# Moving the output stores of seven batches from SyncE's queue to GpSimd's, in a one-core attention and expert kernel

## The chip, the core and the metric

The kernel runs on one core of a Trainium2 chip. The metric is device time in microseconds (us) of one launch, the median of several executions. Engines are named PE (TensorE), DVE (VectorE), ACT (ScalarE), POOL (GpSimd) and SP (SyncE). A DMA is issued from one engine's queue, and a queue takes its instructions in order: an instruction that waits holds back everything behind it on that engine.

## What is computed

There are 8 batches of 576 tokens. Attention (8 heads of 64) first lets 32 learned packs per head attend to the keys and values, and then lets the queries attend to the packed values. The 512 columns that come out per token go to one of 8 experts (two layers, 512 to 1024 to 512), picked per token by a gate, with the previous token's expert kept where a local gate says so:

```python
p_packed = sm_attn(p, k, v)
out = sm_attn(q, p_packed, p_packed)
...
e = fresh_e if s == 0 or local_gate[b, s] < 0.5 else prev_e
h = np.maximum(x[b, s] @ w1[e], 0.0)
out[b, s] = p[e] * (h @ w2[e])
```

## The kernel before

The kernel computes a whole batch with the expert of its first token, and ends with a branch for batches in which some token needs another expert; in the profiled execution the branch isn't taken.

For each batch the second attention's output stays in its factors: weights `a2t` (packs by tokens) and the packed values, which are multiplied into w1 by `pack_weights` (L976), so that layer 1 (L1019) multiplies the attention weights with packed expert weights. Products are made of high and low float32r parts: `a2h` and `a2l` of the attention weights (L688 on ACT, L691 on POOL), `wph` and `wpl` of w1, two halves of `w2s` for w2 (L1005 on ACT, L1007 on DVE, in batch 1 and most of batch 0 on POOL), and two halves of `h` (L1030 on ACT, L1034 on DVE).

Layer 1 and layer 2 run in two halves of the tokens (320 and 256), each over 8 chunks of 128 of the 1024 hidden columns. Layer 2 of a chunk (L1052, L1057, L1061) comes one chunk after its layer 1, and sums in PSUM banks over the 8 chunks. After the last chunk each output block is scaled into a tile `o` and stored (`store`, L1066 to L1101): blocks 0, 1 and 4 at the end of the first half, blocks 2 and 3 at the end of the second. Blocks 0 to 3 are 128 rows of 512 float32 (256 KB), block 4 is 64 rows (128 KB). `o` has 5 buffers. The last batch has other blocks (`LAST_BLOCKS`), cut into smaller stores.

Beside these two layers, PE works ahead on the next batches: scores against the keys (L509), packed values (L573), scores of the queries (L624), the gate (L803, L811), and `pack_weights`. The expert of a batch is found early, in `first_choice` and `first_code` (L755 to L760): DVE writes its number to `e0`, SP reads that into a register (L760, a TENSOR_LOAD) and then issues the expert's w1 in two loads of 1 MB (L926) and w2 in eight of 256 KB (L897). POOL reads the same number (L835), and copies the expert's code to `v0` (L836), which DVE needs for `sel` (L846) in `gates`.

All loads and, before the change, all stores but one of the last batch are issued by SP. Nothing is scheduled on the chip: the order of each engine's instructions is made while the program is built. Generators (`loads`, `weights`, `store`, `gates` and so on) yield the tiles and slots that they need, `weave` steps the one that is due, and a class `Clock` keeps the time at which each engine and each tile would be ready. `Clock.note` books every instruction: a DMA from SP on a resource "DMA" with a rate, a DMA from ACT on a second resource "DMA2" that SP's loads don't share.

Of the kernel before, what the change touches and what calls it, by code (L numbers as in the profile page):

```python
# [19 lines left out]
B, H, S, D = 8, 8, 576, 64  # L20
# [40 lines left out]
class Clock:  # L61
# [71 lines left out]
    def note(self, inst):  # L133
        outs = [x.bass_ap for x in inst.outs if hasattr(x, "bass_ap")]
        ins = [x.bass_ap for x in inst.ins if hasattr(x, "bass_ap")]
        if inst.opcode == "TensorLoad":

            if "SP" in str(inst.engine):
                self.until["SP"] = self.ready([x for x in ins]) + 1000.0
        if not outs:  # L140
            return
        dma = inst.opcode == "DMACopy"
        if dma:
            aside = "Activation" in str(inst.engine)
            kind, took = "DMA2" if aside else "DMA", min(x.free_size() * x.partition_size() for x in outs + ins if x.space != DRAM) * 4 / self.rate
        else:
            kind, took = self.price(inst, outs, ins)
        start = max(self.engine(kind), self.engine("Activation" if aside else "SP") if dma else 0.0)
        for x in ins + ([] if dma else [y for y in outs if y.tensor.name not in self.apart]):
            at, by = self.written.get(self.key(x), (0.0, kind))  # L150
            start = max(start, at + (LAT if by != kind else 0.0 if kind == "PE" else SAME))
        for x in outs:
            t = x.tensor.name
            start = max(start, 0.0 if dma or t in self.apart else self.used.get(self.key(x), 0.0))
            if t in self.before:
                start = max(start, self.used.get(self.before.pop(t), 0.0) + LAT)
        if kind == "Pool" or kind == "DVE" and inst.opcode in ("TensorTensor", "TensorScalar", "TensorScalarPtr") and not any(x.space == PSUM for x in ins + outs):
            for a, z in self.port["DVE" if kind == "Pool" else "Pool"][-8:]:
                if a <= start < z:
                    start = z  # L160
            self.port[kind].append((start, start + took))
        end = start + took
        self.until[kind] = end
        if dma:
            end += 2000.0 if start < 25000.0 else 2500.0
        for x in outs:
            if x.tensor.name in self.apart:
                end = max(end, self.written.get(self.key(x), (0.0, kind))[0])
        for x in outs:
            self.written[self.key(x)] = (end, kind)  # L170
        for x in ins + outs:
            for t in {x.tensor.name, self.key(x)}:
                self.used[t] = max(end, self.used.get(t, 0.0))
# [3 lines left out]
def packed_attn_moe_kernel(  # L177
# [12 lines left out]
    nc = tc.nc  # L190
# [7 lines left out]
    def tile_(shape, dtype, name, tag=None):  # L198
        bufs = BUFS.get(tag or name, 2)
        x = sb.tile(shape, dtype, name=name, tag=tag or name, bufs=bufs)  # L200
        clock.follow(x.tensor.name, tag or name, bufs)
        return x
# [68 lines left out]
    def at(src, b):  # L271

        return src[b] if isinstance(b, int) else src[bass.ds(b, 1)].squeeze(0)
# [8 lines left out]
    def give(*tiles):  # L282
        clock.done.update(x.tensor.name for x in tiles)

    def need(*tiles, slot=(), banks=0, when=None, by=("Activation", "DVE"), first=False, tiled=False):
        slots = [(x, 1) if isinstance(x, str) else x for x in ((slot,) if isinstance(slot, str) else slot)]

        def ready():

            if (when is not None and not when()) or not all(clock.free_slot(*x) for x in slots):  # L290
                return None
            free = free_banks()
            if len(free) < banks + (hold[0] if banks and not first else 0):
                return None
            return max(clock.ready(tiles), free[banks - 1][0] if banks else 0.0, *(clock.slot(*x) for x in slots))
        ready.banks, ready.by, ready.tiled = banks, by, tiled
        return ready
# [742 lines left out]
    def columns(st, i):  # L1040

        return slice(0, DM) if 5 not in st["blocks"][1] or i not in (3, 5) else slice(0, 256) if i == 3 else slice(256, DM)
# [23 lines left out]
    def store(b, st, i, mask=None):  # L1066

        acc, pe = st["acc", i], st["pe"]
        yield need(acc)
        o = tile_([128, DM], F32, "o")  # L1070
        cols, n = columns(st, i), min(i, 3) if i != 4 else 4
        row, rows = ROWS[n]
        if i == 4:

            o2 = tile_([TAIL, DM], F32, "o2", "o")
            nc.scalar.activation(out=o2, in_=acc[TAIL:128], func=AF.Copy, scale=pe[TAIL:128, i:i + 1])
            yield need(o2)
            nc.vector.scalar_tensor_tensor(
                out=o[:TAIL], in0=acc[0:TAIL], scalar=pe[0:TAIL, i:i + 1], in1=o2, op0=ALU.mult, op1=ALU.add,
            )  # L1080
        elif i == 0:

            nc.scalar.activation(out=o[:, 0:256], in_=acc[:, 0:256], func=AF.Copy, scale=pe[:, i:i + 1])
            nc.vector.tensor_scalar(out=o[:, 256:DM], in0=acc[:, 256:DM], scalar1=pe[:, i:i + 1], scalar2=None, op0=ALU.mult)
        elif n == 3:
            nc.scalar.activation(out=o[:, cols], in_=acc[:, cols], func=AF.Copy, scale=pe[:, 3:4])
        else:
            nc.vector.tensor_scalar(out=o, in0=acc, scalar1=pe[:, i:i + 1], scalar2=None, op0=ALU.mult)
        give(acc)
        dst = at(out, b)[row:row + rows]  # L1090
        if mask is not None:
            new, o = o, tile_([128, DM], F32, "o")
            nc.sync.dma_start(out=o[:rows], in_=dst)
            nc.vector.copy_predicated(
                out=o[:rows], mask=mask[:rows, i:i + 1].broadcast_to([rows, DM]), data=new[:rows],
            )
        queue = nc.scalar if i == 5 else nc.sync
        clock.rate = 300.0
        step = rows // 2 if st["blocks"] is LAST_BLOCKS and i in (0, 1, 2, 4) else rows
        for z in range(0, rows, step):  # L1100
            queue.dma_start(out=dst[z:z + step, cols], in_=o[z:z + step, cols])  # L1101
# [173 lines left out]
    with tc.If(stray_reg > 0, label="none_stray"):  # L1275
# [42 lines left out]
        with tc.For_i(0, B) as bi:  # L1318
            with tc.For_i(0, E) as ei:
                go = nc.values_load(todo[0:1, bass.ds(bi, 1), bass.ds(ei, 1)].rearrange("a b e -> a (b e)"), min_val=0, max_val=1)  # L1320
                with tc.If(go > 0):
                    st = {}
# [44 lines left out]
```

## Time and profile before

| | us |
|---|---|
| runs shown, median of 3 | 416.08 |
| runs shown, each | 416.15, 416.08, 412.57 |
| the profiled execution, its own time | 413.3 |
| its span, first to last instruction | 411.5 |
| PE busy / DVE / ACT / POOL | 403.7 / 298.4 / 180.3 / 45.6 |
| mean granted TensorE clock | 1.000 (2.4 GHz) |

The span is what the trace covers; 1.8 us of the profiled execution's time lie outside it. The batches repeat with a period near 47.5 us from 171 us on. Times below are counted from the start of the span. "Idle before" is the time in which an engine waited for the instruction shown, with what released it. Instructions that issue DMAs appear on a queue (SPq), with the time that the issue took.

### The profile page before, as it was taken

Reading aid. Unit: us, or ns where it says so; the run is one execution under the profiler, and the core shown is the slowest. Engines: PE = TensorE matmul, PEld = TensorE weight load, DVE = VectorE, ACT = ScalarE, POOL = GpSimd, SP = SyncE. Lnnn points to the kernel's source line nnn. Section 1 sums busy time; section 2 is a strip of 40 time slices with the busy share of each in tenths; the row PEclk is TensorE's granted clock in tenths of the full one; section 3 lists DMA queues with packets and bytes.
Section 4 is the critical chain, followed back from the end, with each engine's and each line's share of the span. In section 5 each row is a group of like instructions: output and inputs, shape, how many; then the busy total and the mean of one; then the engine's idle time right before and its main releaser. Section 6 shows DMA issues by size and latency. Waiting matters only on the chain.

```text
span 411.5 us, 10035 instructions
## 1 busy us (share of the span) xinstructions
PE 403.7 (98%) x3811; PEld 319.3 (78%) x3817; DVE 298.4 (73%) x905; ACT 180.3 (44%) x440; POOL 45.6 (11%) x67
## 2 busy tenths in 40 slices
PE   7999999999999999999999999999999999999996
PEld 4657777778878788778887788787786788878895
DVE  4497679994969939698687868787695886867231
ACT  3555533643435425455244534364254453454221
POOL 2004400722030000300011000300003000200000
PEclk9999999999999999999999999999999999999999
DMA  7979999999994995859984899829998400744022
GB/s 205 273 266 294 150 168 293 171 280 135 145 364 145 180 168 99 302 153 198 132 256 157 264 132 159 322 87 224 137 139 301 154 2 2 256 141 130 0 65 57
DMA packets 169325, 73.08 MB, mean 178 GB/s; under 512 B 135088, under 2 KB 149424, under 8 KB 169272
## 3 DMA queue, kind: packets, MB, share of 16 engines
q1 hardware_dynamic: 168660, 72.11, 79.1%
q8 instruction: 31, 0.51, 0.6%
q10 hardware_dynamic: 612, 0.28, 0.3%
q14 instruction: 22, 0.18, 0.2%
HBM read 62.94 MB, written 9.44 MB: 176 GB/s over the span
## 4 chain that ended last, share of the span: by engine, by line
PE 84%; DMA 6%; DVE 4%; SPq 3%; issue 1%; ACT 1%; ACTq 0%; DVEq 0%
PE bank L1052 39%; PE bank L1019 22%; PE bank L1057 4%; DMA w1t<-in_moe_w_dram 4%; PE bank L1061 3%; PE bank L976 3%; PE bank L573 2%; PE bank L509 2%; PE bank L624 2%; PE bank L547 2%; DMA p_in<-in_p_dram 1%; PE bank L803 1%; SPq L352 1%; DMA qt<-in_k_dram 1%; SPq L350 1%
## 5 line engine op out<-in xcount | busy, mean ns | idle before, releaser
L1052 PE MATMUL bank<-w2s,h 128*128 128x512 f32 (+1 forms) x792 | 204.3, 392 | 0.5 <-DVE h L1034 0.5
L1052 PEld LDWEIGHTS bank<-w2s,h 128*128 128x128 f32 x792 | 137.3, 188 | 24.4 <-issue 1.7
L1034 DVE SCALAR_TENSOR_TENSOR h<-bank,h 128x256 fp32r<-128x256 f32 x192 | 61.1, 346 | 51.8 <-ACT h L1030 50.7
L1030 ACT ACTIVATE h<-bank 128x256 fp32r<-128x256 f32 (+1 forms) x128 | 52.6, 411 | 104.2 <-PE bank L1019 102.4
L1019 PEld LDWEIGHTS bank<-a2h,wph 128*128 128x128 f32 x256 | 46.6, 188 | 15.4 <-issue 1.8
L1019 PE MATMUL bank<-a2h,wph 128*128 128x320 f32 (+1 forms) x256 | 55.8, 299 | 0.1
L691 POOL TENSOR_TENSOR a2l<-a2t,a2h 128x576 fp32r<-128x576 f32 (+2 forms) x17 | 22.4, 1321 | 297.7 <-ACT a2h L688 297.4
L1019 PE MATMUL bank<-a2h,wpl 128*128 128x320 f32 (+1 forms) x256 | 54.3, 293 | 0.0
L1019 PE MATMUL bank<-a2l,wph 128*128 128x320 f32 (+1 forms) x256 | 54.3, 293 | 0.0
L1019 PEld LDWEIGHTS bank<-a2h,wpl 128*128 128x128 f32 x256 | 40.8, 188 | 0.0
L1019 PEld LDWEIGHTS bank<-a2l,wph 128*128 128x128 f32 x256 | 40.8, 188 | 0.0
L1005 ACT CAST w2s<-w2raw 128x512 fp32r<-128x512 f32 x64 | 37.3, 618 | 1.9 <-DMA w2raw<-in_moe_w_dram 1.7
L1007 DVE TENSOR_TENSOR w2s<-w2raw,w2s 128x512 fp32r<-128x512 f32 x50 | 32.2, 683 | 0.3 <-ACT w2s L1005 0.2
L1057 PE MATMUL bank<-w2s,h 128*128 128x512 f32 x64 | 27.1, 424 | 0.0
L1061 PE MATMUL bank<-w2s,h 128*64 128x512 f32 x64 | 25.3, 395 | 0.0
L644 DVE STREAM_TRANSPOSE sT<-bank 128x288 f32<-128x288 f32 (+2 forms) x36 | 13.1, 418 | 10.2 <-ACT gate L642 9.5
L608 DVE STREAM_TRANSPOSE qn<-qn 128x1152 f32<-128x1152 f32 x14 | 19.2, 1370 | 1.1 <-DMA qn<-in_q_dram 1.0
L1007 POOL TENSOR_TENSOR w2s<-w2raw,w2s 128x512 fp32r<-128x512 f32 x14 | 17.8, 1292 | 15.9 <-ACT w2s L1005 13.0
L989 ACT CAST wph<-bank 128x512 fp32r<-128x512 f32 x28 | 14.7, 598 | 11.0 <-PE bank L976 11.0
L517 DVE TENSOR_SCALAR_CACHE_REDUCE a<-bank 128x288 f32<-128x288 f32 x32 | 13.3, 452 | 5.8 <-PE bank L509 5.8
L992 DVE TENSOR_TENSOR wpl<-bank,wph 128x512 fp32r<-128x512 f32 x28 | 17.3, 669 | 0.0
L476 DVE STREAM_TRANSPOSE qn<-qn 128x1152 f32<-128x1152 f32 x12 | 16.4, 1368 | 0.0
(158 smaller groups left out, 452.2 us busy)
## 6 DMA issues: line engine op xcount, KB each, us to landing
w2raw<-in_moe_w_dram SPq DMA_DIRECT2D x64, 256.0 KB, 6.9
w1t<-in_moe_w_dram SPq DMA_DIRECT2D x14, 1024.0 KB, 7.1
kv<-in_v_dram SPq DMA_DIRECT2D x16, 512.0 KB, 6.1
qn<-in_q_dram SPq DMA_DIRECT2D x28, 288.0 KB, 7.3
out_dram<-o SPq DMA_DIRECT2D x28, 256.0 KB, 3.6
qn<-in_k_dram SPq DMA_DIRECT2D x24, 288.0 KB, 6.0
w1t<-in_moe_w_dram SPq DMA_DIRECT2D x4, 512.0 KB, 3.5
out_dram<-o SPq DMA_DIRECT2D x14, 128.0 KB, 2.4
```

The source lines that it names most:

```text
L476: nc.vector.transpose(out=kT, in_=kT)
L608: nc.vector.transpose(out=qT, in_=qT)
L691: eng.tensor_tensor(out=a2l, in0=a2t, in1=a2h.bitcast(F32), op=ALU.subtract)
L992: nc.vector.tensor_tensor(out=lo[fh][:, Q], in0=ts[fh, Q], in1=hi[fh][:, Q].bitcast(F32), op=ALU.subtract)
L1005: nc.scalar.copy(out=w[:, 0], in_=raw)
L1007: (nc.gpsimd if st["pick"] and not st["early"] or st["early"] and c > 1 else nc.vector).tensor_tensor(out=w[:, 1], in0=raw, in1=w[:, 0].bi ...
L1019: nc.tensor.matmul(out=t[:, :GROUP * (m1 - m0)], lhsT=st["wp"][c // 4][wi][:, Q, fs], rhs=a2[ai][Q][:, GROUP * m0:GROUP * m1], start=(n == ...
L1030: nc.scalar.activation(out=h[:, :w], in_=t[:, :w], func=AF.Relu)
L1034: nc.vector.scalar_tensor_tensor(out=h[:, dst:dst + z - a], in0=t[:, a:z], scalar=0.0, in1=h[:, a:z].bitcast(F32), op0=ALU.max, op1=ALU.su ...
L1052: nc.tensor.matmul(out=acc[:, cols], lhsT=hs[hi], rhs=w[:, wi, cols], start=(c == 0 and n == 0), stop=(c == NC - 1 and n == 2),)
L1057: nc.tensor.matmul(out=acc, lhsT=h[:, 256:WIDE + TAIL], rhs=w[:, 0], start=(c == 0), stop=False, skip_group_check=True,)
L1061: nc.tensor.matmul(out=acc[0:TAIL], lhsT=h[:, 256:WIDE], rhs=w[:, 1], start=False, stop=(c == NC - 1), skip_group_check=True,)
```

## The change

Stores of batches 0 to 6 are issued from POOL's queue; those of the last batch and of the branch stay where they were. These are 35 stores, 28 of 256 KB and 7 of 128 KB. The second edit books them in the planner on "DMA2" and after POOL's own time, where they were on "DMA" after SP's.

```diff
         if dma:
-            aside = "Activation" in str(inst.engine)
+            aside = next((x for x in ("Activation", "Pool") if x in str(inst.engine)), None)
...
-        start = max(self.engine(kind), self.engine("Activation" if aside else "SP") if dma else 0.0)
+        start = max(self.engine(kind), self.engine(aside or "SP") if dma else 0.0)
...
-        queue = nc.scalar if i == 5 else nc.sync
+        queue = nc.scalar if i == 5 else nc.gpsimd if 0 <= st["at"] < B - 1 else nc.sync
```

On SP the three stores of batch 5's first half stood between the load of a later batch's queries (L368) and the register load of batch 6's expert (L760). SP's rows there before:

```order
L368 DMA qn_4155<-in_k_dram 32x72x32 x4
L368 DMA qn_4198<-in_q_dram 32x72x32 x4
L1101 DMA out_0_dram<-o_4493 128x512
L1101 DMA out_0_dram<-o_4499 128x512
L1101 DMA out_0_dram<-o_4513 64x512
L760 TENSOR_LOAD e0_4518
L760 ISA x2
L926 ISA
L926 DMA w1t_4551<-in_moe_w1_dram 128x4x512
```

SP's rows at the same place now:

```order
L368 DMA qn_4164<-in_k_dram 32x72x32 x4
L368 DMA qn_4202<-in_q_dram 32x72x32 x4
L760 TENSOR_LOAD e0_4518
L760 ISA x2
L926 ISA
L926 DMA w1t_4551<-in_moe_w1_dram 128x4x512
```

The register load and the w1 loads now follow directly on the query loads; otherwise SP's loads keep their order, in this place and in the others.

POOL's rows around the gate of batch 2 before (`a2l` are the low parts of batch 2's attention weights, `e0_1800` its expert's number, `v0_2016` the code that DVE's `sel` of batch 2 reads):

```order
L691 TENSOR_TENSOR a2l_1377<-a2t_1373,a2h_1375 128x576
L691 TENSOR_TENSOR a2l_1378<-a2t_1374,a2h_1376 128x576
L835 TENSOR_LOAD e0_1800
L835 ISA x2
L836 ISA
L836 COPY v0_2016<-code_82 128x1
L837 COPY v0_all_114<-v0_2016 128x1
```

POOL's rows there now (`o_1834`, `o_1843` and `o_1854` are blocks 0, 1 and 4 of batch 1, `o_2098` and `o_2109` its blocks 2 and 3):

```order
L1101 DMA out_0_dram<-o_1834 128x512
L1101 DMA out_0_dram<-o_1843 128x512
L1101 DMA out_0_dram<-o_1854 64x512
L691 TENSOR_TENSOR a2l_1377<-a2t_1373,a2h_1375 128x576
L691 TENSOR_TENSOR a2l_1378<-a2t_1374,a2h_1376 128x576
L1101 DMA out_0_dram<-o_2098 128x512
L1101 DMA out_0_dram<-o_2109 128x512
L835 TENSOR_LOAD e0_1800
L835 ISA x2
L836 ISA
L836 COPY v0_2016<-code_82 128x1
```

The copy of `v0` now stands behind two stores, each of which waits for its `o`; from batch 2 on every batch has this order. On DVE the three rows `o_2098` (L1088), `ex` (L844) and `sel` (L846) follow on one another in both kernels. From batch 3 on, the planner also places `pack_weights` and its neighbours on PE one half-step of layer 2 earlier; PE's instructions are the same in number.

## Rows read from the trace of the kernel before

**Rows 1.** The page's first part: busy time and share of each engine, instructions.

```profile
PE 403.7 (98%) x3811; PEld 319.3 (78%) x3817; DVE 298.4 (73%) x905; ACT 180.3 (44%) x440; POOL 45.6 (11%) x67
```

**Rows 2.** Stretches: length, busy us of PE, PEld, DVE, ACT, POOL, PEclk, DMA share, GB/s.

```profile
75.00:125.00 50.00, 49.51 (x486) 39.68 (x486) 39.61 (x108) 22.71 (x56) 15.71 (x16) 1.00 1.14 210
125.00:173.00 48.00, 48.00 (x430) 38.80 (x432) 36.85 (x110) 20.57 (x51) 3.18 (x4) 1.00 0.84 190
...
268.00:318.00 50.00, 49.40 (x487) 39.71 (x480) 38.63 (x114) 22.67 (x55) 3.19 (x4) 1.00 0.88 182
...
365.00:411.50 46.50, 42.55 (x253) 37.42 (x251) 20.46 (x63) 14.09 (x32) 0.00 (x0) 1.00 0.22 61
```

**Rows 3.** Who PE's matmuls waited for: us in total, times, longest.

```profile
PE bank L976 <- DMA w1t<-in_moe_w_dram: 0.6, 1, 0.6
PE bank L1052 <- DVE h L1034: 0.5, 1, 0.5
```

**Rows 4.** Timeline of SP's queue before batch 6's w1: start, us, engine, line, operation.

```profile
301.41 4.21 SPq L1101 DMA_DIRECT2D out_dram<-o  x3
306.69 1.02 SPq L926 DMA_DIRECT2D w1t<-in_moe_w_dram  x2
```

**Rows 5.** Chain of waits that ended last, in the stretch 292 to 320 us.

```profile
302.22 0.15 DVE e L757
...
307.31 7.69 DMA w1t<-in_moe_w_dram
```

**Rows 6.** Timeline of PE at batch 6's `pack_weights`.

```profile
313.35 1.09 PE L976 MATMUL bank<-w1t,ppT 64*32 64x512 f32 x16
315.04 1.09 PE L976 MATMUL bank<-w1t,ppT 64*32 64x512 f32 x16 [0.60 <-DMA w1t<-in_moe_w_dram]
```

**Rows 7.** Timeline of DVE at batch 2's gate.

```profile
131.90 0.73 DVE L1088 TENSOR_SCALAR o<-bank,pe 128x512 f32<-128x512 f32 x1
...
132.65 0.23 DVE L846 TENSOR_SCALAR sel<-code,v 128x8 f32<-128x8 f32 x1
132.78 1.38 DVE L608 STREAM_TRANSPOSE qn<-qn 128x1152 f32<-128x1152 f32 x1
134.08 0.52 DVE L1034 SCALAR_TENSOR_TENSOR h<-bank,h 128x256 fp32r<-128x256 f32 x2
```

**Rows 8.** Timeline of PE at the same time.

```profile
134.18 1.20 PE L509 MATMUL bank<-qn,p_in 64*32 64x288 f32 x32
135.31 0.56 PE L1019 MATMUL bank<-a2h,wph 128*128 128x320 f32 x2
```

**Rows 9.** Line 1101: durations of the issues in ns, least, median and most.

```profile
L1101 SPq DMA_DIRECT2D out_dram<-o x44: 348/485/2999, 61.3 to 407.5; - x44
```

**Rows 10.** Timeline of POOL: its shortest row, `w2s`, two copies of `v0`, `a2l`.

```profile
0.27 0.10 POOL L1353 MEMSET const-float32-0.0<- 128x1 f32 x1
...
77.13 5.24 POOL L1007 TENSOR_TENSOR w2s<-w2raw,w2s 128x512 fp32r<-128x512 f32 x4
...
121.28 0.19 POOL L836 COPY v<-code 128x1 f32 x1
...
308.96 2.95 POOL L691 TENSOR_TENSOR a2l<-a2t,a2h 128x576 fp32r<-128x576 f32 x2 [44.12 <-ACT a2h L688]
311.86 0.18 POOL L836 COPY v<-code 128x1 f32 x1
```

**Rows 11.** Timeline of DVE: the last `o` and `sel`, batches 4 and 7.

```profile
226.41 0.75 DVE L1088 TENSOR_SCALAR o<-bank,pe 128x512 f32<-128x512 f32 x1
...
236.74 0.23 DVE L846 TENSOR_SCALAR sel<-code,v 128x8 f32<-128x8 f32 x1
...
369.58 0.74 DVE L1088 TENSOR_SCALAR o<-bank,pe 128x512 f32<-128x512 f32 x1
...
374.24 0.23 DVE L846 TENSOR_SCALAR sel<-code,v 128x8 f32<-128x8 f32 x1
```

**Rows 12.** Timeline of DVE: one small operation of `gates` in batches 1 and 2.

```profile
78.68 1.25 DVE L828 TENSOR_TENSOR vc<-lt,gmx 128x40 f32<-128x40 f32 x1
...
127.10 0.20 DVE L828 TENSOR_TENSOR vc<-lt,gmx 128x40 f32<-128x40 f32 x1
```

## The prediction

> **What bounds the kernel now.** I read the engines' busy times first. PE is busy 403.7 us of the 411.5 us span [rows 1], so it idles 7.8 us, and nothing done to the other engines can give back more than that. The table of stretches says where those 7.8 us lie: 46.50 - 42.55 = 3.95 us in the last stretch, behind PE's last matmul and in the stores of the last batch, which the change leaves on SP; 0.60 us in 268 to 318 and 0.49 us in 75 to 125; none in 125 to 173 [rows 2]. The rest is at the start, before any store. So what can be won in the middle is about 1.1 us. The list of waits names both: 0.6 us is `pack_weights` waiting for w1, 0.5 us is layer 2 waiting for DVE's `h` [rows 3].
>
> I then followed the 0.6 us back. In batch 6 the second half of `pack_weights` starts at 315.04 after a wait of 0.60 us for w1 [rows 6]. The chain has that transfer from 307.31 for 7.69 us, and the expert's number, on which it depends, done by DVE at 302.22 + 0.15 = 302.37 [rows 5]. Between the two SP was at three stores, from 301.41 to 305.62, and only then came to the register load and to w1 at 306.69 [rows 4]. The last of the three stores waits for a block that DVE writes after the expert's number, and SP can't pass it. That is the wait that the change removes.
>
> **The change part by part.** *SP loses 35 stores.* With the median issue of 0.485 us [rows 9] that is 17 us of SP's time, but SP's time as such is worth nothing: PE doesn't wait for SP except as shown. What counts is that w1 leaves sooner. In batch 6 the register load can go at about 302.4 and w1 some 0.6 us later, since 306.69 - 305.62 = 1.1 us is what it takes at most; 303 against 306.69 is 3.6 us earlier, far more than the 0.6 us that PE waited and the half-step of layer 2 by which `pack_weights` is planned earlier. So -0.6 us. In the other batches PE shows no wait for w1, and an earlier w1 gives nothing.
>
> *POOL gains 35 stores.* It is busy 45.6 us [rows 1], so there is room; what matters is what stands behind a store. Two things do: `a2l` and the copy of `v0`. The `a2l` of batch 6 start at 308.96 and waited for ACT [rows 10], while the stores in front have their blocks by then, since SP had issued the last of them by 305.62 [rows 4]; even if the last block came only at 305.62, one store behind it may take 3.3 us. No cost.
>
> The copy of `v0` is the other case. Before, POOL copied `v0` long before DVE asked: at 121.28 for batch 2 [rows 10], and `sel` ran at 132.65 [rows 7]. Now the copy stands behind the stores of the previous batch's blocks 2 and 3, and those wait for `o`, which DVE writes from 131.90 to 132.63. DVE asks for `v0` 0.02 us later. So in batch 2 DVE must sit through two store issues on POOL and a copy of 0.19 us. In batch 4 (3, 5 and 6 have the same distance) `sel` comes 236.74 - 227.16 = 9.6 us after `o`, in batch 7 it is 374.24 - 370.32 = 3.9 us [rows 11]. In those the stores fit.
>
> No row shows what a store issued from POOL takes there. The nearest by kind is SP's issue, median 0.485 us; by engine it is a POOL operation over 128 rows of 512, 5.24 / 4 = 1.31 us. The ends are POOL's shortest row, 0.10 us, and the longest store issue on SP, 3.0 us [rows 9, 10]. The two nearest are close together, and I take their middle, 0.9 us. Then DVE stands for 2 x 0.9 + 0.19 = 2.0 us in batch 2. Queued behind `sel` on DVE are a transpose (L608, 1.38 us) and L1034 of a layer 1 product. PE's next layer 1 (L1019 at 135.31) takes over the PSUM bank that this L1034 reads, and L1034 ended at 134.08 + 0.52 = 134.60 [rows 7, 8]. So the slack is 0.7 us, and PE loses 2.0 - 0.7 = 1.3 us. After that DVE is no later than PE, and the loss isn't paid twice. At 0.10 us a store DVE stands 0.4 us and PE loses nothing. At 3.0 us it stands 6.2 us: PE loses 5.5 us in batch 2, and in batch 7 6.2 - 3.9 - 0.7 = 1.6 us more, 7.1 us together.
>
> The Trainium skill (DMA: Bandwidth & Descriptors, Specifications) gives about 1 us to the first byte from GpSimd's queue and about 0.6 us from SyncE's, and advises SyncE for a plain store. By that ratio a store would take an estimated 0.8 us and PE lose 1.1 us in place of 1.3 us.
>
> *The planner books stores elsewhere.* The order on PE changes from batch 3 on, but not the instructions, and PE had no idle time there to fill [rows 2]. I cost it at nothing; what hides an error here is the 3.6 us by which w1 is early. If a load that the planner now believes in is late, it would show as a PE wait of the size seen already, 0.6 us a batch.
>
> **Sum.** Against the profiled execution: 413.3 - 0.6 + 1.3 = 414.0 us, which is +0.7. That execution is 2.8 us below the median of 416.08, and the four known executions are 412.57, 413.3, 416.08 and 416.15, two near each of two levels. Their mean is 414.5, so I put the forecast at 414.5 + 0.7 = 415.2 us. About 1% (4.2 us) is what a measurement of this kernel can tell from no change; this is far inside.
>
> **The rivals.** *Stores on POOL hold DVE up everywhere (slower).* POOL and DVE do get in each other's way in this trace: a DVE operation of 128x40 takes 1.25 us at 78.68, beside POOL's `w2s` (77.13 to 82.37), and 0.20 us at 127.10 with POOL idle [rows 10, 12]. So one POOL instruction can hold DVE for 1.05 us. If a store does that too, each batch has a cluster of three and one of two, against a slack of 0.7 us. If every second store meets such an operation, a batch loses 1.6 - 0.7 and 1.05 - 0.7, 1.2 us, and seven batches 8.7 us: 424 us. With a third of them it is 0.35 us a batch, 2.5 us, 417.7 us. It decides from about two hits in five, where the loss passes 1%. For it speak the row, and many small DVE operations beside the stores. Against it: a store only issues a transfer, while `w2s` reads and writes 128x512 of SBUF.
>
> The Trainium skill (SBUF — State Buffer, Who interferes with whom) has a rule on this: a DVE operation with two SBUF inputs contends with a GpSimd instruction that reads SBUF, not with one that only writes, and descriptor writing is blocked only by DVE's two-port modes. With it the trace agrees as far as `w2s` goes (1.25 us against 0.20), and by it the 128x40 operation wouldn't be held by a store. That lowers this rival; small scalar operations remain exposed.
>
> *w1 was late more often than the profile shows (faster).* Batch 6 waited 0.6 us with w1 under way for 7.69 us. If the executions at 416 are those in which each of six batches waits about as long, the change gives back 3.6 us and more: from 415.2, 411.6 us. For it: the two levels. Against it: only one batch of the profile waits at all.
>
> *It doesn't do what it says.* If SP is held by slots for w2 or by the transfers in front, w1 isn't earlier, the 0.6 us stay, and the time is 415.8 us. The rows speak against it: SP was at stores until 305.62.
>
> **How the numbers follow.** Forecast 0.60, SP not freed 0.14; both are within 1%, 0.74 together. DVE held up, or a store near its upper end, slower by over 1%: 0.17. w1 late in many batches, faster by over 1%: 0.09. The range goes down to 411.5 us (the lowest run, 412.57, less the 1.1 us that PE can win) and up to 421.5 us, which takes in stores of 3.0 us (415.2 + 7.1 - 1.3 = 421.0) and the milder half of the slow rival.
>
> **What would show it.** Right: w1 of batch 6 issued near 303 and no wait of L976 for w1; a DVE wait of about 2 us before `sel` at about 132.7, released by POOL's copy, and a PE wait of about 1.3 us before a layer 1 product near 136; PE's idle time in 173 to 268 still near none. Wrong: DVE operations drawn out wherever POOL issues stores; PE waits in every batch; `a2l` late for layer 1; w1 issued no earlier than before.

## The result, and the profile after

The changed kernel takes 416.26 us (median of 13 executions, 415.13 to 421.92) against 413.65 us for the kernel before in the same session (13 executions, 412.57 to 416.15). The ratio of the means, without the one execution of 421.92 us, which ran in a slower state, is 1.0067, with a 95% interval of 1.0038 to 1.0097: 2.8 us slower (1.6 to 4.0). The forecast was 415.2 us and no change that can be told; the time lies inside the range that was given, but the change of +0.7 us on which it rested lies below the interval. A second, independent comparison (e10 below) gave 1.0058 (1.0021 to 1.0095).

The profiled execution of the changed kernel took 418.28 us, its span is 416.5 us. The page's first part, as in [rows 1]:

```profile
PE 406.9 (98%) x3816; PEld 321.9 (77%) x3817; DVE 296.5 (71%) x905; ACT 179.3 (43%) x440; POOL 67.4 (16%) x102
```

The stretches, as in [rows 2] (the last row now ends at 416.5):

```profile
75.00:125.00 50.00, 48.87 (x462) 38.80 (x454) 39.80 (x110) 22.40 (x54) 18.84 (x19) 1.00 1.15 206
125.00:173.00 48.00, 46.96 (x449) 38.45 (x434) 35.83 (x110) 21.38 (x52) 4.71 (x10) 1.00 0.85 176
268.00:318.00 50.00, 50.00 (x474) 40.33 (x475) 39.34 (x114) 21.67 (x53) 7.79 (x10) 1.00 0.87 202
365.00:416.50 51.50, 46.70 (x323) 39.91 (x322) 21.37 (x65) 16.55 (x37) 1.48 (x4) 1.00 0.20 61
```

POOL has 35 instructions more, the stores, and is busy 21.8 us longer, 19.4 of them in the stores. PE now idles 1.13 us in 75 to 125 (0.49 before) and 1.04 us in 125 to 173 (none before), nothing in 268 to 318 (0.60 before), and 4.80 us in the last stretch (3.95 before). The list of PE's waits names them, against [rows 3]:

```profile
PE bank L1019 <- DVE h L1034: 1.0, 1, 1.0
PE bank L1052 <- DVE h L1034: 0.7, 2, 0.5
...
PE bank L1019 <- DVE a L517: 0.4, 1, 0.4
```

Of the 0.7 us for L1052, 0.5 are the wait that [rows 3] has too.

To add up what each place costs, one needs marks that both kernels have. PE's instructions are the same, so I take the starts of four PE rows in the timeline, and the lengths between them:

- **A**, batch 1: from L509 (x32, at 86.70 before) to the first L573 behind it (97.43).
- **V**, around batch 2's gate: from L509 (x32, at 134.18 before) to the first L573 behind it (147.19).
- **W**, around batch 6's w1: from L573 (289.49 before) to the next batch's L509 (327.04).
- **T**, the tail: from the end of PE's last matmul to the end of the span. **S**: the start of the first layer 1 product.

| us | A | V | W | T | S |
|---|---|---|---|---|---|
| before, profile on record | 10.73 | 13.01 | 37.55 | 3.95 | 28.66 |
| before again (e9) | 10.73 | 13.01 | 37.00 | 4.43 | 28.91 |
| before again (e15) | 10.73 | 13.01 | 36.72 | 3.96 | 28.94 |
| after, profile on record | 11.90 | 14.09 | 36.75 | 4.80 | 31.47 |
| after again (e10) | 11.94 | 14.09 | 36.74 | 4.39 | 28.74 |
| after again (e16) | 12.23 | 14.08 | 36.75 | 4.85 | 29.29 |

A and V repeat to some hundredths of a us where nothing waits, so they are far sharper than the times. In the means of the three profiles A costs +1.29, V +1.08, T +0.57, and W gives back 0.34 us: +2.6 us together, beside 2.8 and 2.4 us measured. S varies, and is told of at the end.

That agreement is looser than it looks. All that lies between S and PE's end is 2.3 us longer in the mean: A, V and W make 2.0 of it, and ahead of A another 0.5 us comes and goes with the execution (in e16 PE waits 0.54 us for batch 1's w1). With T and with S, 1.0 us later in the mean, the three profiles of the changed kernel are 3.9 us longer than the three of the kernel before.

**Batch 2's gate (V)** went as forecast. DVE and then POOL at the place of [rows 7] and [rows 10]:

```profile
136.18 0.19 DVE L844 TENSOR_TENSOR ex<-lt,gmx 128x40 f32<-128x40 f32 x1
138.01 0.23 DVE L846 TENSOR_SCALAR sel<-code,v 128x8 f32<-128x8 f32 x1 [1.65 <-POOL v L836]
138.16 1.37 DVE L608 STREAM_TRANSPOSE qn<-qn 128x1152 f32<-128x1152 f32 x1
139.46 0.51 DVE L1034 SCALAR_TENSOR_TENSOR h<-bank,h 128x256 fp32r<-128x256 f32 x2
...
136.56 1.11 POOL L1101 DMA_DIRECT2D out_dram<-o  x2 [11.53 <-DVE ex L844]
137.80 0.18 POOL L836 COPY v<-code 128x1 f32 x1
...
140.12 0.53 PE L1019 MATMUL bank<-a2h,wph 128*128 128x320 f32 x2 [1.04 <-DVE h L1034]
```

POOL can store only when DVE has written `o` (its wait is put down to L844, the instruction behind the one that wrote `o`); two issues of 1.11 us together and the copy later, `sel` may run. DVE waits 1.65 us, and PE 1.04 us for the L1034 behind it. The issues and the copy are 1.29 of the 1.65 us; the rest lies between DVE's L844 and POOL's first store, between the last store and the copy, and between the copy and `sel`.

**Batch 6's w1 (W)** went as forecast too: the w1 loads leave at 308.01, before the last store on POOL at 308.84, and `pack_weights` runs as one row without a wait, where [rows 6] has two and a wait of 0.60 us between them. Counted from the start of W, w1 leaves at 13.67, 13.65 and 13.67 us in the three profiles of the changed kernel, and at 17.20, 16.65 and 15.65 us in those of the kernel before: up to 3.5 us earlier, where 3.6 were forecast.

```profile
308.01 1.03 SPq L926 DMA_DIRECT2D w1t<-in_moe_w_dram  x2
...
308.84 0.55 POOL L1101 DMA_DIRECT2D out_dram<-o  x1 [1.11 <-DVE o L1078]
...
317.52 1.95 PE L976 MATMUL bank<-w1t,ppT 64*32 64x512 f32 x32
```

**Batch 1 (A)** was not in the forecast. The timeline of the kernel before, DVE and then POOL:

```profile
87.81 0.20 DVE L859 TENSOR_TENSOR ex<-ex,sel 128x40 f32<-128x40 f32 x1
87.92 0.17 DVE L862 TENSOR_SCALAR gz<-gz 128x5 f32<-128x5 f32 x1
88.00 1.37 DVE L608 STREAM_TRANSPOSE qn<-qn 128x1152 f32<-128x1152 f32 x1
...
91.61 1.07 DVE L864 TENSOR_SCALAR gsm<-gsm 128x5 f32<-128x5 f32 x1
...
90.09 5.04 POOL L1007 TENSOR_TENSOR w2s<-w2raw,w2s 128x512 fp32r<-128x512 f32 x4 [7.35 <-ACT w2s L1005]
```

And of the changed kernel, DVE, POOL, PE:

```profile
90.34 0.55 DVE L859 TENSOR_TENSOR ex<-ex,sel 128x40 f32<-128x40 f32 x1
90.81 1.29 DVE L862 TENSOR_SCALAR gz<-gz 128x5 f32<-128x5 f32 x1
92.01 1.36 DVE L608 STREAM_TRANSPOSE qn<-qn 128x1152 f32<-128x1152 f32 x1
...
89.53 2.53 POOL L1007 TENSOR_TENSOR w2s<-w2raw,w2s 128x512 fp32r<-128x512 f32 x2
...
93.79 0.56 PE L1019 MATMUL bank<-a2h,wph 128*128 128x320 f32 x2 [0.42 <-DVE a L517]
...
95.63 1.20 PE L1052 MATMUL bank<-w2s,h 128*128 128x512 f32 x4 [0.22 <-DVE h L1034]
```

L862 works on 128x5 and takes 1.29 us in place of 0.17, L859 0.55 in place of 0.20: 1.47 us more, with POOL's `w2s` beside them. In the kernel before `w2s` begins after these two, and holds up L864 instead (1.07 us), for which nobody waits. DVE's L608 and L517 come behind L862, and PE waits for L517 and then for `h`. The two waits shown make 0.64 us, A 1.17: a wait is counted from the modelled end of the matmul before it, which the next matmul otherwise overlaps (before, L1061 at 90.44 for 0.39 us and the next L1019 at 90.68), and the first matmuls behind a wait start further apart. The length of the stretch is the cost, not the sum of the listed waits.

### The profile page after: what moved, and what is told of

Same layout as the page of the kernel before. It is cut to its first block, busy times and chain, and to the rows that moved or that the text cites. A ratio compares the mean times of both kernels' runs of the same rounds, so it can differ in the third digit from the quotient of the medians.

```text
span 416.5 us, 10073 instructions
## 1 busy us (share of the span) xinstructions
PE 406.9 (98%) x3816; PEld 321.9 (77%) x3817; DVE 296.5 (71%) x905; ACT 179.3 (43%) x440; POOL 67.4 (16%) x102
## 4 chain that ended last, share of the span: by engine, by line
PE 84%; SPq 4%; issue 4%; DVE 3%; DMA 3%; ACT 1%; POOL 1%; POOLq 0%; DVEq 0%; ACTq 0%
PE bank L1052 37%; PE bank L1019 21%; PE bank L1057 4%; PE bank L1061 3%; SPq L368 3%; PE bank L573 2%; PE bank L976 2%; PE bank L547 2%; PE bank L624 2%; PE bank L509 2%; PE bank L231 2%; DMA qn<-in_q_dram 2%; PE bank L454 1%; DMA kw<-in_k_dram 1%; DVE qn L608 1%
## 5 line engine op out<-in xcount | busy, mean ns | idle before, releaser
L1052 PE MATMUL bank<-w2s,h 128*128 128x512 f32 (+1 forms) x792 | 203.9, 392 | 0.7 <-DVE h L1034 0.7
L1052 PEld LDWEIGHTS bank<-w2s,h 128*128 128x128 f32 x792 | 137.9, 188 | 25.4 <-DVE h L1034 1.6
L1034 DVE SCALAR_TENSOR_TENSOR h<-bank,h 128x256 fp32r<-128x256 f32 x192 | 61.0, 345 | 54.0 <-ACT h L1030 53.5
L1019 PEld LDWEIGHTS bank<-a2h,wph 128*128 128x128 f32 x256 | 46.6, 188 | 17.1 <-issue 2.4
L1019 PE MATMUL bank<-a2h,wph 128*128 128x320 f32 (+1 forms) x256 | 56.0, 300 | 1.5 <-DVE h L1034 1.0
L1101 POOL DMA_DIRECT2D out_dram<-o x35 | 19.4, 554 | 234.6 <-DVE o L1084 137.5
L1019 PE MATMUL bank<-a2h,wpl 128*128 128x320 f32 (+1 forms) x256 | 54.4, 294 | 0.0
L1019 PE MATMUL bank<-a2l,wph 128*128 128x320 f32 (+1 forms) x256 | 54.4, 294 | 0.0
L1019 PEld LDWEIGHTS bank<-a2h,wpl 128*128 128x128 f32 x256 | 40.9, 188 | 0.0
L1019 PEld LDWEIGHTS bank<-a2l,wph 128*128 128x128 f32 x256 | 40.8, 188 | 0.0
L1007 DVE TENSOR_TENSOR w2s<-w2raw,w2s 128x512 fp32r<-128x512 f32 x50 | 31.9, 683 | 0.8 <-ACT w2s L1005 0.6
L1061 PE MATMUL bank<-w2s,h 128*64 128x512 f32 x64 | 25.3, 395 | 0.0
L608 DVE STREAM_TRANSPOSE qn<-qn 128x1152 f32<-128x1152 f32 x14 | 19.2, 1368 | 0.5 <-DMA qn<-in_q_dram 0.5
L1007 POOL TENSOR_TENSOR w2s<-w2raw,w2s 128x512 fp32r<-128x512 f32 x14 | 17.8, 1292 | 9.0 <-ACT w2s L1005 6.1
```

Source lines behind the costliest of these rows:

```text
L608: nc.vector.transpose(out=qT, in_=qT)
L1007: (nc.gpsimd if st["pick"] and not st["early"] or st["early"] and c > 1 else nc.vector).tensor_tensor(out=w[:, 1], in0=raw, in1=w[:, 0].bi ...
L1019: nc.tensor.matmul(out=t[:, :GROUP * (m1 - m0)], lhsT=st["wp"][c // 4][wi][:, Q, fs], rhs=a2[ai][Q][:, GROUP * m0:GROUP * m1], start=(n == ...
L1034: nc.vector.scalar_tensor_tensor(out=h[:, dst:dst + z - a], in0=t[:, a:z], scalar=0.0, in1=h[:, a:z].bitcast(F32), op0=ALU.max, op1=ALU.su ...
L1052: nc.tensor.matmul(out=acc[:, cols], lhsT=hs[hi], rhs=w[:, wi, cols], start=(c == 0 and n == 0), stop=(c == NC - 1 and n == 2),)
L1061: nc.tensor.matmul(out=acc[0:TAIL], lhsT=h[:, 256:WIDE], rhs=w[:, 1], start=False, stop=(c == NC - 1), skip_group_check=True,)
```

## The experiments

After reading both traces I held theory A: the loss is three terms that come from the stores on POOL, namely the two stores in front of `v0`; POOL's `w2s` of batch 1, pulled forward because SP, free of stores, loads w2 earlier; and a longer tail; less the gain of w1. The rivals are named in the expectations.

Every edit keeps the kernel's arithmetic. Where the order of the other engines was to stay that of the one kernel while the stores were issued as in the other, a field `clock.book` tells the planner what to book a store as, whichever queue issues it. "SP's order" below is a store booked as before, "POOL's order" one booked as in the changed kernel.

**e1, the planner's order alone.** All stores from SP, booked as POOL's.

```diff
-        queue = nc.scalar if i == 5 else nc.gpsimd if 0 <= st["at"] < B - 1 else nc.sync
+        queue = nc.scalar if i == 5 else nc.sync
...
+            clock.book = "Pool" if i != 5 and 0 <= st["at"] < B - 1 else None
```

> All 35 stores are issued by SP as before, but the planner books them as if POOL issued them; the order of PE, DVE and ACT is that of the changed kernel. Theory A (the loss is three terms that come from the stores on POOL: v0 of batch 2 +1.1, POOL's w2s of batch 1 on DVE +1.1, end waits +0.8, less 0.7 for w1): with the stores on SP all of them are gone, so no PE wait of L1019 at v0 in batch 2, none behind L517 in batch 1, the tail behind PE's last matmul near 3.95 us, and at most a w1 wait of 0 to 0.6 us; the time is within 0.8 us of the kernel before. Rival B (the planner's other order costs the time): 2 to 3 us over the kernel before, with PE waits in batches 3 to 6.

Measured: 1.0083 (1.0051 to 1.0114), no store on POOL. A is 12.12, V 13.01, W 37.59, T 4.02 us. So theory A was wrong in one of its terms: the loss in batch 1 comes with the planner's order, not with the queue. Rival B was right in that, but the waits are not in batches 3 to 6. The ratio is 3.4 us (2.1 to 4.7), more than A's 1.4 us; in the profile 0.8 us more lie ahead of A, and the rest was not followed. The rows in batch 1, POOL, DVE, PE:

```profile
88.13 2.54 POOL L1007 TENSOR_TENSOR w2s<-w2raw,w2s 128x512 fp32r<-128x512 f32 x2 [4.47 <-DMA w2raw<-in_moe_w_dram]
...
88.72 0.75 DVE L859 TENSOR_TENSOR ex<-ex,sel 128x40 f32<-128x40 f32 x1
89.40 1.30 DVE L862 TENSOR_SCALAR gz<-gz 128x5 f32<-128x5 f32 x1
...
92.39 0.56 PE L1019 MATMUL bank<-a2h,wph 128*128 128x320 f32 x2 [0.64 <-DVE a L517]
```

The order of PE and DVE at this place is the same in both kernels, but ACT's is not (buffer numbers left out):

```
before:  L1030 h | L1030 h | L1005 w2s x3 | L538 a | L1030 h | L1005 w2s
after:   L1030 h | L1005 w2s x2 | L1030 h | L1005 w2s x2 | L538 a | L1030 h
```

With batch 0's stores no longer booked on the loads' resource, the planner has w2 there earlier (e5, which books these stores as SP's again, has the order of before) and puts two of ACT's casts one `h` forward. POOL's L1007, which needs the casts, follows, and meets L859 and L862.

**e2, the queue alone.** All 35 stores from POOL as in the change, booked as SP's.

```diff
+            clock.book = "SP" if i != 5 and 0 <= st["at"] < B - 1 else None
```

> All 35 stores are issued by POOL, but the planner books them as SP's, so that PE, DVE and ACT keep the order of the kernel before. Theory A: the v0 wait of batch 2 (DVE 1.5 to 2 us, PE about 1 us), the w2s of batch 1 on DVE (PE about 0.6 us in two waits near 94 to 96 us) and the longer tail (4.8 us) all stay, the w1 wait is gone; 1.5 to 3 us over the kernel before. Rival B (planner): within 0.5 us of the kernel before, or faster.

Measured: 1.0048 (1.0013 to 1.0084). A 10.74, V 14.08, W 36.72, T 4.84. The wait for `v0` and the gain of w1 belong to the queue; batch 1's loss is absent, though SP is as free as in the changed kernel.

**e3, batch 1's last two stores back on SP.** POOL's order.

```diff
-        queue = nc.scalar if i == 5 else nc.gpsimd if 0 <= st["at"] < B - 1 else nc.sync
+        queue = nc.scalar if i == 5 else nc.gpsimd if 0 <= st["at"] < B - 1 and (st["at"], i) not in ((1, 2), (1, 3)) else nc.sync
```

> The changed kernel, but blocks 2 and 3 of batch 1 go out from SP; nothing else in any order changes. Theory A: DVE's wait before sel in batch 2 (1.65 us) and PE's before L1019 (1.04 us) are gone, the rest stays: 1.0 us less than the changed kernel, about 1.6 us over the kernel before. Rival C (the loss is spread over all stores on POOL, and DVE is held up for another reason): the wait stays or comes up at the next store, no more than 0.2 us less.

Measured: V is 13.00, that of the kernel before, and DVE goes through without a stop; A stays at 12.23. The two stores in front of the copy are what costs 1.08 us. The ratio, 1.0067 (1.0035 to 1.01), shows no gain, and the profile says why most of it is lost again: in batch 2 DVE now waits for one of POOL's stores before it may write block 4, and PE behind it.

```profile
163.71 0.74 DVE L1078 SCALAR_TENSOR_TENSOR o<-bank,pe,o 64x512 f32<-64x512 f32 x1 [1.11 <-DMA out_dram<-o]
...
164.84 1.20 PE L1052 MATMUL bank<-w2s,h 128*128 128x512 f32 x4 [0.43 <-DVE h L1034]
```

From the L509 at the start of V to the next such row it is 50.44 us, against 50.80 in the changed kernel and 49.68 in the kernel before: of the 1.08 us only 0.36 are won. So rival C has a point, a wait does come up at the next stores. Why DVE waits for that store, the runs don't show.

**e4, batch 0's stores back on SP.** POOL's order.

```diff
-        queue = nc.scalar if i == 5 else nc.gpsimd if 0 <= st["at"] < B - 1 else nc.sync
+        queue = nc.scalar if i == 5 else nc.gpsimd if 1 <= st["at"] < B - 1 else nc.sync
```

> The changed kernel, but the five stores of batch 0 go out from SP, which holds batch 1's second four w2 loads back behind them as before; the order of PE, DVE and ACT is that of the changed kernel. Theory A: POOL's second four w2s of batch 1 (L1007) start about 3 us later relative to PE, DVE's L859 and L862 take 0.2 us each again, and PE's waits for L517 and L1034 near 94 to 96 us are gone: 0.6 to 1.1 us less than the changed kernel. Rival C (the stores themselves, or another cause in batch 1): the waits stay, no change. Rival D (the contention only moves to another operation that PE needs): L859 and L862 are short, but as much PE idle time comes up within 10 us.

Measured: 1.0065 (1.0034 to 1.0095), A 11.86. The waits stay, as e1 lets one expect: holding SP's loads back doesn't help as long as ACT has the casts early. Theory A's account of this term, that earlier loads pull POOL's work forward, is refuted.

From here on theory A2 has the planner's casts in its place.

**e5, both undone.** The changed kernel, with batch 0's stores booked as SP's, and batch 1's last two issued by SP by the queue line of e3.

```diff
+            clock.book = None if i == 5 or not 0 <= st["at"] < B - 1 else "Pool" if st["at"] > 0 else "SP"
```

> The changed kernel with batch 0's five stores booked by the planner as SP's (they still go out from POOL), which puts ACT's casts of batch 1's second four w2s back behind h, and with blocks 2 and 3 of batch 1 issued by SP. Theory A2 (two of the losses are: the planner's earlier casts in batch 1, +1.2 us from L509 to L573 of that stretch, wherever the stores are issued; the two late stores of batch 1 in front of v0, +1.1 us): both stretches are as in the kernel before within 0.1 us, w1 still gains 0.8 us, the tail still costs 0.85 us; 2.3 us less than the changed kernel, within 0.5 us of the kernel before. Rival E (some of the loss is in what all 35 stores on POOL do together): more than 1 us over the kernel before remains.

Measured: 1.0026 (0.9993 to 1.0059). A 10.73, V 13.01, W 36.74: both stretches are those of the kernel before. Behind V the wait of e3 comes again (PE 0.43 us). Batch 1's `pack_weights` waited 0.8 us for w1 in this execution; e11, with all stores on SP, shows the same (0.9 us), so it needs no store on POOL. The ratio is 1.1 us over the kernel before (-0.3 to 2.4): A and V are explained by their two causes, but rival E, that something of all the stores on POOL remains, is not excluded.

**e6 and e7, only the three stores in front of batch 6's w1,** on POOL and on ACT, in SP's order. The edit of e6; e7 has `nc.scalar` for `nc.gpsimd`:

```diff
-        queue = nc.scalar if i == 5 else nc.sync
+        queue = nc.scalar if i == 5 else nc.gpsimd if st["at"] == 5 and i in (0, 1, 4) else nc.sync
```

> The kernel before, in its order, with three stores alone on POOL: blocks 0, 1 and 4 of batch 5, those in front of batch 6's w1. Theory A2: L976's wait for w1 in batch 6 goes, 0.8 us from L573 to L509 there. Tail, theory A2 (a fixed cost once POOL has issued any DMA): 4.8 us behind PE's last matmul, so the sum is 0. Rival F (it grows with the stores): 4.0 to 4.2 us, so 0.6 us faster than before.

> The same three stores on ACT's queue, which has issued DMAs in the kernel before too. Theory A2: w1's 0.8 us are won as with POOL, and the tail stays at 3.95 us: 0.8 us faster than the kernel before. Rival G (ACT waits at a store for the block that DVE writes, and holds back the relu of layer 1, L1030): PE waits about 0.5 to 1 us for h near the stores, and nothing or less is won.

Measured: POOL 1.0023 (0.999 to 1.0055), W 36.72, T 5.15. ACT 1.0029 (0.9996 to 1.0062), W 37.58, T 4.58. On ACT the store of block 4 stands between two `h`, the second of these comes late, and PE waits 0.60 us: w1's wait is only replaced. ACT and PE in the timeline of e7:

```profile
302.75 0.69 ACT L1076 ACTIVATE o<-bank,pe 64x512 f32<-64x512 f32 x1 [1.97 <-DVE e L757]
303.46 0.69 ACT L667 ACTIVATE sT<-sT 128x576 f32<-128x576 f32 x1
304.24 0.56 ACTq L1101 DMA_DIRECT2D out_dram<-o  x1
304.84 0.38 ACT L1030 ACTIVATE h<-bank 128x256 fp32r<-128x256 f32 x1 [0.70 <-PE bank L1019]
...
305.28 0.96 PE L1052 MATMUL bank<-w2s,h 128*128 128x512 f32 x3 [0.60 <-ACT h L1030]
```

As to the tail: SP ends the program with a run of semaphore waits on L1362. Its rows, first the kernel before, then the changed one, then e6 (least, median and most in ns, first and last start):

```profile
L1362 SPq EVENT_SEMAPHORE  x10: 17/28/28, 410.2 to 411.5; - x10
```

```profile
L1362 SPq EVENT_SEMAPHORE  x14: 17/28/28, 414.8 to 416.4; - x14
```

```profile
L1362 SPq EVENT_SEMAPHORE  x12: 17/28/28, 410.4 to 411.8; - x12
```

Ten waits take 1.3 us, twelve 1.4, fourteen 1.6: some 0.1 us for each wait that POOL's stores add. In the other profiles ten take 1.2 or 1.3 us (but 1.6 in e12) and fourteen 1.5 or 1.6. The rest of T varies from execution to execution with the last stores (3.95 to 4.80 in kernels without a store on POOL), so neither A2's fixed 0.85 us nor rival F's 4.0 to 4.2 us is borne out; about 0.3 us can be put down to the change.

**e8, POOL held back in batch 1.** The changed kernel with six memsets ahead of POOL's L1007 there, which the planner doesn't book; in essence:

```diff
+            if st["at"] == 1 and c == 4: [nc.gpsimd.memset(heat, 1.0) for _ in range(6)]
             (nc.gpsimd if st["pick"] and not st["early"] or st["early"] and c > 1 else nc.vector).tensor_tensor(out=w[:, 1], ...
```

> The changed kernel with six memsets of a dead 128x512 bf16 tile on POOL ahead of its second four w2s in batch 1, which the planner does not book: POOL's w2s start about 2.5 us later, no other engine's order changes. Theory A2 (POOL's w2s beside DVE's small operations L859 and L862 is what costs 1.2 us): L859 and L862 take 0.2 us each again, PE's waits for L517 and L1034 near 94 and 96 us go, 1.2 us less than the changed kernel. Rival H (the other order on ACT costs it): PE's waits stay. Rival I (memsets that only write hold DVE too): L862 stays at about 1.3 us.

Measured: A is 10.73, exactly that of the kernel before, with ACT's other order still in place; V 14.08 as expected; 1.0044 (1.0006 to 1.0082). POOL and DVE:

```profile
89.62 3.46 POOL L226 MEMSET heat<- 128x512 bf16 x6
93.05 5.04 POOL L1007 TENSOR_TENSOR w2s<-w2raw,w2s 128x512 fp32r<-128x512 f32 x4
...
90.45 0.20 DVE L859 TENSOR_TENSOR ex<-ex,sel 128x40 f32<-128x40 f32 x1
90.56 0.21 DVE L862 TENSOR_SCALAR gz<-gz 128x5 f32<-128x5 f32 x1
```

For batch 1 this settles it: it is POOL's `w2s` beside L859 and L862, not ACT's order as such, and memsets, which only write, hold neither of the two up.

**e9 and e10, both kernels again.**
Neither has an edit.

> The kernel before once more, unchanged. Theory A2: the start varies from execution to execution (first layer 1 product 28.7 to 31.6 us in the ten profiles so far, whatever the kernel), so this profile may start up to 3 us later too; between that product and PE's end all stretches agree with the first profile within 0.3 us, but for waits on loads (0.6 to 0.8 us). Rival J (the kernel before has the early start, the changed ones a late one): 28.7 again. Ratio 1.000 within 0.4%.

> The changed kernel once more, unchanged. Theory A2: between the first layer 1 product and PE's end it again loses 1.2 us in batch 1 and 1.1 us in batch 2 and wins 0.8 us in batch 6; SP's last run of semaphore waits counts 14 and takes 1.6 us in place of 10 and 1.3 us. Ratio 1.004 to 1.009.

Measured: before 0.9978 (0.9942 to 1.0015); after 1.0058 (1.0021 to 1.0095). The stretches are in the table above. New is W: in the kernel before it is 37.55, 37.00 and 36.72 us in three profiles, and in e9 PE waited 0.8 us for w1 in two other places. What the change gives back by an earlier w1 thus lies between nothing and 0.8 us in batch 6, depending on when w1 leaves in the kernel before.

**e11 and e12, w1 ahead of the stores on SP.** The kernel before; the stores of the first half of batch 5 (e12: of batches 2 to 6) wait in the planner until the next batch's w1 loads are issued.

```diff
+        yield need(when=lambda: not (st["at"] == 5 and i in (0, 1, 4)) or len(sts[st["at"] + 1].get("w1", ())) > 1)
         queue = nc.scalar if i == 5 else nc.sync
```

> The kernel before, all stores on SP, but the three stores of batch 5's first half are issued behind batch 6's register load and w1 loads. Theory A2: batch 6's w1 wait goes without POOL, 0.6 to 0.8 us from L573 to L509 there, no v0 wait, no earlier casts in batch 1, 10 end waits: 0.7 us faster than the kernel before. Rival B (the planner's order changes behind it, since the loads are now booked earlier, and costs as in batch 1): a wait of 0.5 us or more comes up after batch 5, and nothing is won.

> As the run before, with the stores of the first half of batches 2 to 6 behind the next batch's w1 loads. Theory A2: as that run, since no other batch waits for w1 in the profile; 0.7 us faster than the kernel before. If w1 was late in other executions in other batches too, more: up to 0.7 us for each. Rival B: waits of 0.5 us or more per batch from the planner's other order.

Measured: 1.0022 (0.9989 to 1.0055) and 1.0027 (0.9992 to 1.0062). In e11 W is 36.75, so the wait is won as expected, but the planner's order changes behind it, and PE waits in batch 7 where it didn't:

```profile
368.36 0.41 PE L1019 MATMUL bank<-a2h,wpl 128*128 128x320 f32 x1 [0.27 <-DVE wpl L992]
368.95 0.41 PE L1019 MATMUL bank<-a2h,wpl 128*128 128x320 f32 x1 [0.18 <-DVE wpl L992]
```

From the end of W to PE's end e11 takes 81.7 us, the kernel before 80.5. In e12 the same two waits come in an earlier batch, and one of 0.44 us for w1. Nothing is won; rival B was right. No version was found that beats the kernel before.

**e13 to e16** went after the start, S. e13 has all 35 stores on ACT, in POOL's order; e14 those of batches 4 to 6 on POOL, in SP's order; e15 and e16 have no edit.

```diff
-        queue = nc.scalar if i == 5 else nc.gpsimd if 0 <= st["at"] < B - 1 else nc.sync
+        queue = nc.scalar if i == 5 else nc.scalar if 0 <= st["at"] < B - 1 else nc.sync
```

```diff
-        queue = nc.scalar if i == 5 else nc.gpsimd if 0 <= st["at"] < B - 1 else nc.sync
+        queue = nc.scalar if i == 5 else nc.gpsimd if 4 <= st["at"] < B - 1 else nc.sync
```

> All 35 stores on ACT's queue, with the planner's order of the changed kernel on PE, DVE and SP. Start: theory K (a kernel with many stores on POOL loads its first k later, before any store is issued: PE's second group of L454 starts at 6.35 us or later in all seven such profiles, at 6.28 or earlier in all seven others) expects 6.1 to 6.3 us, as POOL issues nothing; rival L (chance) has no say. Batch 1: the planner's earlier casts cost 1.2 us as in the changed kernel. Batch 2: no v0 wait. w1 of batch 6: won, but ACT waits at stores and holds back the relu of layer 1 (0.6 us as seen with three stores, up to that per batch, 4 us in all): slower than the kernel before by 2 to 5 us.

> The kernel before, in its order, with the 15 stores of batches 4, 5 and 6 on POOL. No v0 wait in batch 2, no earlier casts in batch 1, w1 of batch 6 won (0.6 to 0.8 us), SP's last run of semaphore waits 14 (8 lanes of POOL or as many as before, 12 with three stores). Theory K with a dose: second group of L454 between 6.25 and 6.45 us; rival L: anywhere from 6.1 to 6.6 us. Time within 0.5 us of the kernel before if the start is early, up to 2 us over it if late.

> The kernel before, one look at its start. Theory K: second group of L454 at 6.1 to 6.3 us, first layer 1 product at 28.5 to 29.1 us. Rival L (the late start comes by chance in half of all executions): 6.4 us or later and 30 to 31.6 us as likely as not.

> The changed kernel, one look at its start. Theory K: second group of L454 at 6.35 us or later, first layer 1 product at 28.7 to 31.6 us, later than 29.2 us in five of seven. Rival L: as likely as not at 6.1 to 6.3 us.

Measured: e13 1.0289 (1.0233 to 1.0344), much worse than I expected. Its list of PE's waits, beside those above:

```profile
PE bank L1052 <- ACT h L1030: 4.2, 6, 1.5
...
PE bank L1019 <- DVE h L1034: 1.7, 5, 0.8
...
PE bank L1019 <- DVE a L517: 1.1, 1, 1.1
```

Six batches show the wait of e7, once with 1.50 us. The six of e7's kind make 4.2 us and those of L1019 and L517 2.8 us, of 12 us between the first layer 1 product and PE's end. The other 5 us are not all followed; as in A, a listed wait is less than what it costs: from the L509 at 241.59 to the next such row it takes 48.79 us, the kernel before 47.45, with 0.75 us of listed waits in between. e14: 1.000 (0.9967 to 1.0033), A, V and W at 10.73, 13.01 and 36.71. As for the start, theory K asked for PE's second group of L454 at 6.1 to 6.3 us in e13 and at 6.35 or later in e16; they came at 6.89 and 6.17. K is refuted in both.

## Why the prediction was wrong, point by point

The forecast's change was -0.6 us for w1 and +1.3 us for `v0`. Measured are -0.34 (W) and +1.08 (V), and two terms that the sum doesn't have: +1.29 (A) and some +0.3 in the tail.

**SP loses 35 stores: the mechanism right, the size not stable.** W shows the 0.6 us term as 0.8 us in the profile on record, but as 0.3 and 0.0 us in two further profiles of the kernel before. One profile of a wait for a DMA is one draw; the mean gain in batch 6 is 0.34 us. In the same way "in the other batches PE shows no wait for w1" held for that profile and not for e9.

**POOL gains 35 stores, the copy of v0: right, a little less.** A store of POOL takes 0.54 us, not 0.9 (the row below); DVE waits 1.65 us, not 2.0, PE 1.04, not 1.3. That these are so near is in part luck: with 0.54 us the forecast's own sum gives 2 x 0.54 + 0.19 = 1.27 us for DVE and 0.6 for PE; it had nothing for the gaps between the engines, and the store that was taken too long made up for them. That `a2l` costs nothing and that batches 3 to 7 have room was right: there is no PE wait from 173 us to the tail.

```profile
L1101 POOL DMA_DIRECT2D out_dram<-o x35: 539/542/693, 64.4 to 375.2; - x35
```

The Trainium skill (DMA: Bandwidth & Descriptors, Specifications) has about 1 us for GpSimd's queue; that is to the first byte, and the time that an issue holds POOL, 0.54 us here, is another quantity, nearer to SP's issue.

**The planner books stores elsewhere, "I cost it at nothing": this is the step that failed.** It measures +1.2 to +1.5 us (A), about half of the whole loss. The working looked at PE's order, found the same instructions and no idle time, and stopped. But the planner orders ACT too, whose order was not read, and there two casts had moved in batch 1. I had the second half of the mechanism in hand: a small DVE operation beside POOL's `w2s` takes 1.25 us instead of 0.20 [rows 12], and the first rival was built on it. I asked whether a store holds DVE up in that way, and not whether the change moves `w2s` itself. e1 and e2 separate planner and queue, e8 shows POOL's `w2s` beside the small operations to be the cause.

**The first rival** (stores on POOL hold DVE up) is refuted: in e2 all stores are on POOL, and A as well as the batches behind V are as in the kernel before. The rule of the Trainium skill that was cited for it (SBUF — State Buffer, Who interferes with whom) agrees with the rows of e8 and of the change: L859, with two inputs in SBUF, is held up by `w2s`, which reads, and not by memsets, which only write. L862, the larger part of the loss, has one input and is no case of the rule as it was cited.

**The other two rivals.** That w1 would leave no earlier is refuted by W. That w1 was late in many batches (faster) did not come out: e9 has waits for w1 in two batches, 0.8 us together, but the changed kernel has one too (e16, 0.54 us), and the time rose.

**The tail**: the prediction had none of it. Four more semaphore waits at the end cost some 0.3 us; the rest of T varies.

**The base**: 414.5 us, the mean of four known executions, stands against 413.65 us in the session of the result. That alone hid 0.9 us of the loss, so that the time looks nearer to the forecast than the change is. And a measurement tells more than the 1% that was assumed: its interval here is 0.3% to either side, so 2.8 us is a change that can be told.

## What to carry to other kernels

When a program is ordered by a planner, an edit to its books is a change to every engine: compare the order of each engine, ACT and POOL too, before costing it at nothing, and look whether a POOL operation that reads SBUF moves beside short DVE operations on the path. Where a change is worth under 1%, measure stretches between fixed instructions; A and V of the kernel before repeat to 0.01 us in three profiles, where its times differ by 3.6 us. Moving a store to another queue doesn't take its wait away: a store waits for its block on whichever engine issues it, and holds back what stands behind it there, a load on SP, a copy on POOL, an `h` on ACT. Where nothing urgent stands behind it, it costs nothing that shows (e14: 1.000).

## What was unexpected

**Five columns on DVE can cost PE a us.** A 128x5 operation took 1.29 us in place of 0.17 beside POOL's 128x512 subtraction, and with L859 it cost PE 1.2 us (A).

**The start comes in two kinds, and its cause stays open.** S lies between 28.5 and 29.3 us, or between 30.0 and 31.6. In the late ones PE's matmuls around 9 to 12 us take about twice as long. The same row in the changed kernel's profile on record (S 31.47) and in e10, the same program (S 28.74):

```profile
10.18 1.97 PE L454 MATMUL bank<-ident,kw 128*128 128x128 f32 x8
```

```profile
8.63 1.09 PE L454 MATMUL bank<-ident,kw 128*128 128x128 f32 x8
```

In three of the late profiles, e2, e5 and e13, the granted clock from 9 to 11 us is 0.50, the lower of the two levels, 1.2 GHz; before it fell PE had waited 0.85 to 0.88 us for a k. In the other three, the changed kernel's on record, e4 and e8, the clock reads 1.00 while the matmuls take as long, and they have not been faster before: the second group of L454 takes 1.11 or 1.12 us, in the early profiles 0.66 to 0.91. That stretch in e2 and in the changed kernel's profile on record, columns as in [rows 2]:

```profile
9.00:11.00 2.00, 2.00 (x16) 1.74 (x9) 1.00 (x5) 0.59 (x1) 0.00 (x0) 0.50 0.93 233
```

```profile
9.00:11.00 2.00, 2.00 (x21) 1.05 (x21) 0.75 (x4) 0.00 (x0) 0.00 (x0) 1.00 0.96 241
```

Late starts came in five of eight profiles of kernels with 30 or more stores on POOL, in e13, and in none of the nine others. No store is issued before 60 us, and e10 and e16 show early starts of the changed kernel itself, so this may be chance; the runs don't settle it. No term above rests on it, but if the later start is the change's, the account lacks a term of up to 1 us, the difference of the means of S.
